# State products moved in a PE-bound scan and MLP kernel: ahead of the scans in the first group, into the y tile of the pair before in the later ones

## The chip, the cores and the metric

One core of one Trainium2 chip. The time is the device time of one execution in microseconds; the figure of a kernel is the median of its runs. A profile is one such execution, and its span is somewhat shorter than the execution's own time.

## The reference, cut to what matters

```python
# x (4, 8, 768, 32), a (4, 8, 768), B and C (4, 8, 768, 16); chunks of 32 steps
for c in range(nc):
    cum = np.cumsum(log(a) of the chunk)
    L = exp(cum_i - cum_j), causal
    y_intra = ((Cc @ Bc.T) * L) @ xc
    y_inter = (Cc @ state) * exp(cum)
    y[chunk] = y_intra + y_inter
    state = decay_full * state + sum_j(Bc_j xc_j * decay_from_j)
h = y_as_tokens(3072, 256) @ w_in          # (256, 2048)
g = maximum(h, 0) + alpha * minimum(h, 0)
out = g @ w_out                            # (2048, 256)
```

The result doesn't depend on the length of a chunk; the kernel takes 128 steps to a chunk. The weights arrive as 64-bit floats.

## The kernel before, in words

**Units of work.** There are 24 chunks of 128 steps (4 sequences of 6), taken two at a time: 12 pairs, `gp` 0 to 11. Two pairs make a group of 512 tokens, so there are six groups, and three pairs make a sequence. A pair first gives y for its 256 tokens; the MLP then runs on whole groups. In the third pair of each sequence (2, 5, 8, 11) only the first chunk's state is needed, since the sequence ends there.

**A pair** is a Python generator, `pair(gp)` (line 416). Each `yield` ends a step, and `ssm(gp, stages)` takes so many steps. In the order of the kernel before, for pairs 4 to 11 (`fine` is true there):

- transposes of B and C (L469), ACT's copy of them to `bc` (L472), and `bn`, B scaled by decays, by POOL (`pair_loads`, L385)
- four steps of decay scans on DVE (`half_decays`, L438), two scans each, with ACT's `spread_c` (L484: C spread to `cz`) in the fourth
- the state products (`added`, L519) on PE into a PSUM tile of their own, the state on DVE (`states`, L547), its masked copy `sm` on POOL (L550), and POOL's `c_decayed` (L487)
- Gram products of B and C (L564) and their multiplication with the decays on DVE (L600), in two steps
- y (L616 with the states, L623 with the decayed Gram), two PSUM tiles, each copied to `xts` by ACT (L630)

Pairs 0 and 1 start the kernel and have an order of their own. Pairs 2 and 3 run in the loop of the first group, with all scans of a chunk in one step; before, they have seven steps: transposes with `spread_c` and `bn`; scans of the first chunk; scans of the second; state products; Gram, first half; Gram, second half; y.

**The first group's MLP** is direct: `hidden` (L642, with ACT's multiply L645 and DVE's L646 as the PReLU) for each of 16 blocks of 128 columns, and `output` (L680). The first four blocks are taken in halves by `hidden_two` (L657, L663, L669). The loop over `f` from 4 to 15 runs, at each `f`, the steps of pairs 2 and 3, `hidden(0, f)`, one weight conversion, and `output(f - 4)`.

**The weights** come as 16 pieces of 512 KB, alternating `w_in` and `w_out` (piece 3 is the first of `w_out`, piece 4 serves blocks 6 and 7, piece 5 is the second of `w_out`). Of each, `convert_a` issues ACT's two reads of the raw piece (L218, L225 or L228) and POOL's clip (L220); `convert_b` two DVE operations (L238, L239); `convert` the add that finishes it (L261, mostly POOL). `convert_next` converts the next piece, issues `convert_a` for the piece after the next unless `first=False`, and issues the load of the piece six later on SP.

**The later groups** multiply by a seven-product scheme with sums: `quad(g, z, after)` takes four blocks at a time (z 0 to 3) in PSUM tiles A and Y (L766), PReLUs (L749, L751), POOL's differences (L800, L809), and `product` (L741) multiplies the quad before by `w_out`. It needs sums of weights (`weight_sums`, L709) and of tokens (`token_sums`, four operations on POOL, L721). `after(j)` is called at 14 places in a quad; a table, `steps`, says at which (z, j) a pair takes a step, and `ahead` at which `pair_loads` is called for a later pair. With `nxt = 2 * g + 2`, pairs `nxt` and `nxt + 1` are worked in group g's quads, for the group after.

**Order.** Every engine runs its instructions in the order in which the program issues them, so a place in the program is a place in each engine's queue. PSUM has eight banks: two for `ps_s` (tag `ss`), two for `ps_h` (tag `hp`: hidden tiles, A, Y, and spare ones), four `bank(i)` for outputs. In the first group `ss_tile` takes turns between the two of `ps_s` and `bank(2)`, once `bank(3)` holds an identity for the scans (`identity_bank`). The fourth Gram block of a pair takes an `hp` tile (`spare`).

Of the kernel before, what the change touches and what calls it, by code (L numbers as in the profile page):

```python
# [9 lines left out]
F32 = mybir.dt.float32  # L10
U32 = mybir.dt.uint32
U16 = mybir.dt.uint16
ALU = mybir.AluOpType
# [9 lines left out]
def kernel(  # L23
# [25 lines left out]
    nc = tc.nc  # L49
# [6 lines left out]
    P = 128  # L56
# [52 lines left out]
    def ss_tile():  # L109
        if early[0] is None:  # L110
            return ps_s.tile([P, 512], F32, name="ss")
        early[0] += 1
        i = early[0] % (3 if ident_p else 4)
        return ps_s.tile([P, 512], F32, name="ss") if i < 2 else bank(i)
# [211 lines left out]
    held = {}  # L326
    bns = {}

    def identity_bank():


        m5_bank.append(bank(3))
        nc.scalar.copy(out=m5_bank[0][:, HT:], in_=ident_h[:, :HT])
        ident_p.append(m5_bank[0][:, HT:])
# [42 lines left out]
    def pair_loads(gp):  # L377

        b, c = divmod(2 * gp, CPB)
        nat, abc, xt, ap = loads["p", gp]  # L380

        bn = work.tile([P, 2, H * N], F32, name="bn")
        i, bi = divmod(b, 2)
        pj = prt[i].rearrange("p (b h c) -> p b c h", b=2, h=H)[:, bi, c : c + 2]
        nc.gpsimd.tensor_tensor(  # L385
            out=bn.rearrange("p k (h n) -> p k h n", h=H),
            in0=nat[:, 0].rearrange("p k (h n) -> p k h n", h=H),
            in1=pj.unsqueeze(3).to_broadcast([P, 2, H, N]), op=ALU.mult)
        return bn
# [22 lines left out]
    def spare():  # L412

        return ps_h.tile([P, GT], F32, name="hp", tag="hp")

    def pair(gp):

        b, c = divmod(2 * gp, CPB)
        nat, abc, xt, ap = loads["p", gp]
        last = c + 2 == CPB  # L420
        dec = work.tile([P, 2, H, Q], F32, name="dec")
        dv = dec.rearrange("p k h t -> p k (h t)")

# [37 lines left out]
            yield  # L461


        tp = spare() if gp == 1 else ss_tile()
        if gp == 0:
            keep_warm(tp, 3, Q)
# [10 lines left out]
        def spread_c():  # L477
            for e in range(2):
                o = cz[:, e].rearrange("p k t -> p (k t)")
                if gp == 0 and e == 1:  # L480
                    nc.gpsimd.tensor_scalar(out=o, in0=ct, scalar1=par[:, e : e + 1],
                                            scalar2=None, op0=ALU.mult)
                else:
                    nc.scalar.mul(o, ct, par[:, e : e + 1])  # L484

        def c_decayed():
            nc.gpsimd.tensor_tensor(out=cd.rearrange("p k t -> p (k t)"), in0=ct, in1=pf,  # L487
                                    op=ALU.mult)

        fine = gp >= 2 * GC // 2  # L490
        if not fine:
            spread_c()
        if gp == 0:
            rows_turn(0, held.pop("pr"))
            dps = spare()
            keep_warm(dps, 6, Q)
            yield
        bn = bns.pop(gp) if gp in bns else pair_loads(gp)
        if gp == 1:
            c_decayed()  # L500
            dps = spare()
# [1 line left out]
        elif gp:  # L503
            yield

        nk = 1 if last else 2
        st = [masked.get(b)]  # L510
        new = work.tile([P, 2, P], F32, name="state")
        sm = work.tile([P, 2, P], F32, name="sm")

        def added(dps):
            dps = dps.rearrange("p (k m) -> p k m", m=P)
            for k in range(nk):
                for w in range(KC):
                    ws = slice(64 * w, 64 * w + 64)
                    nc.tensor.matmul(dps[ws, k], bn[:, k, ws], xt[:, k, w * P : (w + 1) * P],  # L519
                                     start=True, stop=True, tile_position=(0, 64 * w),  # L520
                                     skip_group_check=True)
            return dps

        if fine:
            for k in range(2):
                for w in range(2):
                    half_decays(k, w)
                    if k == 1 and w == 1:
                        spread_c()
                    yield  # L530
        else:
            decays(0)
            if gp == 1:
                dps = added(dps)
            if gp:
                yield
            if gp != 1:
                decays(1)

        def states(dps):  # L540
            for k in range(nk):
                old = state.get(b)
                if old is None:
                    nc.scalar.copy(out=new[:, k], in_=dps[:, k])
                else:
                    e = (k + 1) * Q - 1
                    nc.vector.scalar_tensor_tensor(out=new[:, k], in0=old, scalar=pf[:, e : e + 1],  # L547
                                                   in1=dps[:, k], op0=ALU.mult, op1=ALU.add)
                state[b] = new[:, k]
            nc.gpsimd.tensor_tensor(out=sm[:, :nk], in0=new[:, :nk],  # L550
                                    in1=hmask.unsqueeze(1).to_broadcast([P, nk, P]), op=ALU.mult)
            st.extend(sm[:, k] for k in range(nk))
            masked[b] = st[-1]

# [21 lines left out]
        if gp == 0:  # L578
            gram = products_bc()
            dps = added(dps)  # L580
            yield
            c_decayed()
            times(dec[:, :, :2], one_less(gram))
        elif gp == 1:
            decays(1)
            gram = products_bc()
            g0 = one_less(gram)
            states(dps)
            times(dec[:, :, :2], g0)
        else:  # L590
            if not fine:
                yield
            states(added(ss_tile()))
            c_decayed()
            yield
            gram = products_bc()
        for i, r in enumerate(r for r in ((2, 3, 0, 1) if fine else (3, 2, 1, 0) if gp > 1 else range(4))
                              if r in gram):
# [6 lines left out]
        yield  # L605


        y = [ss_tile()[:, : 2 * Q].rearrange("p (k t) -> p k t", k=2) for w in range(KC)]
        if gp < 2:
            keep_warm(y[0].rearrange("p k t -> p (k t)"), 2 - gp)  # L610
        begun = False
# [347 lines left out]
    prelus[1]()  # L959
    ssm(1)  # L960
    convert_a(*pieces[3])
    prelus = [hidden_two(0, 0, 2 * Q, spare())]
    prelus[0]()
    prelus = [hidden_two(0, 2, 2 * Q, spare())]
    convert_a(*pieces[4])
    convert_next(first=False)
    prelus[0]()
    identity_bank()
    convert_a(*pieces[5])
    convert_next()  # L970
    in_steps = {8: 0, 10: 1, 12: 2, 14: 3}
    for f in range(FIRST, NF):
        if f in (5, 10):
            load_pair(3 + f // 10)
        if f == 5:
            load_rows(1)
        if f == 9:
            rows_clamp(1)
            held["pr"] = rows_scan(1)
            rows_out(1)  # L980
        if f <= 10:
            ssm(2)
        if f >= 9:
            ssm(3)
        hidden(0, f)
        convert_next()
        output(f - FIRST)
        if f in in_steps:
            weight_sums(wi, in_sums, 0, in_steps[f])
    early[0] = None  # L990
    token_sums(1)
    ssm(2 * GC // 2, 2)


    steps = {(0, 1): 0, (0, 2): 0, (0, 5): 0, (0, 9): 0, (0, 13): 0, (1, 1): 0, (1, 5): 0,
             (1, 12): 1, (1, 14): 1, (2, 1): 1, (2, 2): 1, (2, 5): 1, (2, 9): 1, (2, 13): 1,
             (3, 1): 1, (3, 5): 1, (3, 12): 2, (3, 14): 2}

    late_sums = {(0, 2): ((wqt, out_sums, 0, 0),), (0, 4): ((wqt, out_sums, 0, 1),),
# [11 lines left out]
    for i in range(NZ * (NG - 1)):  # L1011
        g, z = divmod(NZ + i, NZ)
        nxt = 2 * g + 2

        def after(j, g=g, z=z, i=i, nxt=nxt):
            places = with_gram if nxt < NP and z % 2 == 0 else without
            if i and j in places:
                product(*divmod(NZ + i - 1, NZ), places[j])
            if i == 0:
                for f, half in last_out.get(j, ()):  # L1020
                    output(NF - LATE + f, half)
            if (i, j) in ((0, 13), (1, 8)):
                store_first(i)
            for w, sums, q0, part in late_sums.get((i, j), ()):
                weight_sums(w, sums, q0, part)
            if g > 1 and z == 0 and j in (5, 9, 13, 14):
                if j == 5:
                    comb[0] = combine(g - 1)
                next(comb[0], None)
            if g > 1 and z in (1, 3) and j == 11:  # L1030
                finish(g - 1, z // 2)
            if nxt + steps.get((z, j), NP) < NP:
                ssm(nxt + steps[z, j])
            if nxt < NP and (z, j) == (3, 7):
                token_sums(g + 1)
            ahead = nxt + {(1, 3): 1, (3, 8): 2}.get((z, j), NP)
            if ahead < NP:
                if ahead == 6:
                    rows_turn(1, held["pr"])
                bns[ahead] = pair_loads(ahead)  # L1040

        comb = [None] if i == 0 else comb
        if z == 0 and nxt < NP:
            load_pair(nxt + 1)
        if z == 2 and nxt + 2 < NP:
            load_pair(nxt + 2)
        quad(g, z, after)
# [31 lines left out]
```

## Time and profile before

| what | value |
|---|---|
| median of 10 runs | 378.34 us (377.33 to 379.7) |
| the profiled execution | 378.65 us |
| its span | 376.9 us |
| start of the loop over `f` on PE (hidden of block 4) | 31.21 us |
| first quad of the second group on PE | 86.24 us |

Each row of a group or of the timeline gives the engine, the source line, the operation, what is written and read, and the count. In the timeline the first two columns are start and duration in us, and the bracket at the end says how long the engine idled ahead of the row and on what. A row of waits gives the waiting engine and line, the releaser, the total in us, how often, and the longest.

### The profile page before, as it was taken

Reading aid. Unit: us, or ns where it says so; the run is one execution under the profiler, and the core shown is the slowest. Engines: PE = TensorE matmul, PEld = TensorE weight load, DVE = VectorE, ACT = ScalarE, POOL = GpSimd, SP = SyncE. Lnnn points to the kernel's source line nnn. Section 1 sums busy time; section 2 is a strip of 40 time slices with the busy share of each in tenths; the row PEclk is TensorE's granted clock in tenths of the full one; section 3 lists DMA queues with packets and bytes.
Section 4 is the critical chain, followed back from the end, with each engine's and each line's share of the span. In section 5 each row is a group of like instructions: output and inputs, shape, how many; then the busy total and the mean of one; then the engine's idle time right before and its main releaser. Section 6 shows DMA issues by size and latency. Waiting matters only on the chain.

```text
span 376.9 us, 6178 instructions
## 1 busy us (share of the span) xinstructions
PE 365.8 (97%) x2223; PEld 294.5 (78%) x2223; DVE 242.4 (64%) x461; ACT 179.7 (48%) x384; POOL 203.4 (54%) x212
## 2 busy tenths in 40 slices
PE   8898899999999999999999999999999999999996
PEld 7675466668778788788788788788788788888884
DVE  7884799967637737747737847647856734543364
ACT  1557766525354445545435535525625525543541
POOL 4875366779766846445456345356364355264512
PEclk9999999999999999999999999999999999999999
DMA  7989698831008801001801801801811000001003
GB/s 144 222 163 343 181 242 211 170 77 56 30 0 162 174 2 54 4 0 28 168 17 31 178 2 29 181 1 28 152 33 22 9 0 15 16 0 30 1 0 84
DMA packets 121879, 30.71 MB, mean 81 GB/s; under 512 B 93737, under 2 KB 117753, under 8 KB 121849
## 3 DMA queue, kind: packets, MB, share of 16 engines
q1 hardware_dynamic: 116736, 29.74, 35.7%
q10 hardware_dynamic: 5112, 0.59, 1.1%
q8 instruction: 17, 0.28, 0.3%
q14 instruction: 14, 0.11, 0.1%
HBM read 26.98 MB, written 3.34 MB: 80 GB/s over the span
## 4 chain that ended last, share of the span: by engine, by line
PE 87%; DVE 5%; DMA 2%; POOL 2%; ACT 2%; issue 1%; POOLq 0%; DVEq 0%; ACTq 0%
PE hp L766 33%; PE bank L741 32%; PE bank L680 5%; PE hp L642 3%; DMA raw<-in_moe_w_in_dram 2%; PE ss L623 2%; PE ss L564 2%; PE ss L616 1%; DVE dec L438 1%; PE ss L519 1%; PE hp L564 1%; PE hp L657 1%; PE ss L469 1%; PE hp L270 1%; DVE wr L239 1%
## 5 line engine op out<-in xcount | busy, mean ns | idle before, releaser
L809 POOL TENSOR_TENSOR gt<-gt 128x512 f32<-128x512 f32 x58 | 73.6, 1269 | 31.7 <-DVE gt L751 24.8
L751 DVE SCALAR_TENSOR_TENSOR gt<-hp,s_mul,gt 128x256 f32<-128x256 f32 x120 | 52.6, 480 | 47.7 <-ACT gt L749 46.7
L741 PE MATMUL bank<-gt,w_out 128*128 128x256 f32 x320 | 82.5, 382 | 0.4 <-ACT o_sb L687 0.4
L749 ACT ACTIVATE gt<-hp,s_alpha 128x256 f32<-128x256 f32 x120 | 50.3, 470 | 47.2 <-PE hp L766 32.9
L741 PEld LDWEIGHTS bank<-gt,w_out 128*128 128x128 f32 x320 | 60.0, 190 | 11.2 <-issue 2.3
L800 POOL TENSOR_TENSOR gt<-gt 128x512 f32<-128x512 f32 x20 | 25.4, 1270 | 78.3 <-DVE gt L751 78.3
L741 PE MATMUL bank<-gt,ws 128*128 128x256 f32 x240 | 58.3, 379 | 0.0
L741 PEld LDWEIGHTS bank<-gt,ws 128*128 128x128 f32 x240 | 45.1, 190 | 5.8
L438 DVE TENSOR_TENSOR_SCAN dec<-abc,bank 128x256 f32<-128x256 f32 x80 | 48.1, 661 | 0.0
L766 PE MATMUL hp<-xs,w_in 128*128 128x256 f32 x160 | 42.8, 390 | 0.0
L766 PE MATMUL hp<-xT,w_in 128*128 128x256 f32 x160 | 41.9, 384 | 0.0
L766 PE MATMUL hp<-xs,ws 128*128 128x256 f32 x160 | 41.1, 379 | 0.0
L785 DVE TENSOR_TENSOR hp<-hp,u 128x512 f32<-128x512 f32 x20 | 14.0, 700 | 39.6 <-ACT u L783 39.6
L774 ACT COPY m<-hp 128x512 f32<-128x512 f32 x20 | 11.7, 586 | 51.5 <-PE hp L766 51.5
L766 PEld LDWEIGHTS hp<-xs,w_in 128*128 128x128 f32 x160 | 28.7, 189 | 7.7 <-issue 3.3
L766 PEld LDWEIGHTS hp<-xs,ws 128*128 128x128 f32 x160 | 30.4, 190 | 4.1
L766 PEld LDWEIGHTS hp<-xT,w_in 128*128 128x128 f32 x160 | 29.7, 190 | 5.0 <-issue 1.4
L680 PEld LDWEIGHTS bank<-w_out,gt 128*128 128x128 f32 x128 | 24.1, 190 | 11.7 <-issue 4.9
L680 PE MATMUL bank<-w_out,gt 128*128 128x256 f32 x128 | 30.7, 381 | 2.3 <-POOL w_out L261 2.3
L789 DVE TENSOR_TENSOR c<-hp,m 128x512 f32<-128x512 f32 x20 | 13.6, 682 | 19.3 <-PE hp L766 19.3
L642 PE MATMUL hp<-xT,w_in 128*128 128x512 f32 x48 | 23.3, 607 | 0.7 <-DVE gt L646 0.7
L783 ACT COPY u<-hp 128x512 f32<-128x512 f32 x20 | 11.7, 585 | 23.0 <-PE hp L766 23.0
(155 smaller groups left out, 555.4 us busy)
## 6 DMA issues: line engine op xcount, KB each, us to landing
abc<-z SPq DMA_DIRECT2D x20, 512.0 KB, 5.0
raw<-in_moe_w_in_dram SPq DMA_DIRECT2D x8, 512.0 KB, 5.2
raw<-in_moe_w_out_dram SPq DMA_DIRECT2D x8, 512.0 KB, 6.9
xt<-in_x_dram SPq DMA_DIRECT2D x24, 128.0 KB, 3.2
out_dram<-o_sb SPq DMA_DIRECT2D x32, 64.0 KB, 1.9
nat<-in_B_dram SPq DMA_DIRECT2D x22, 64.0 KB, 2.8
nat<-in_C_dram SPq DMA_DIRECT2D x22, 64.0 KB, 3.6
ap<-pf SPq DMA_DIRECT2D x11, 128.0 KB
```

Of the source, the lines that this page charges most:

```text
L438: nc.vector.tensor_tensor_scan(out=dv[:, k, hs], data0=abc[k][:, hs], data1=ident_p[0], initial=0.0, op0=ALU.mult, op1=ALU.add)
L642: nc.tensor.matmul(hp, w_in[:, k, f * P : (f + 1) * P], xts[g][:, k], start=(k == 0), stop=(k == KC - 1))
L680: nc.tensor.matmul(pos[0][t // 2][:, t % 2], gt[:, t * Q : (t + 1) * Q], w_out[:, f], start=(f == 0 and t % 2 == 0), stop=(f == NF - 1), s ...
L741: nc.tensor.matmul(ms[g][i][:, h], w, blocks[g, z][n][:, p], start=(q == 0 and h == 0), stop=(q == NQ - 1), skip_group_check=True)
L749: nc.scalar.mul(o[:, p], h[:, p], s_alpha[:, fs[p]])
L751: nc.vector.scalar_tensor_tensor(out=o[:, p], in0=h[:, p], scalar=s_mul[:, fs[p]], in1=o[:, p], op0=ALU.mult, op1=ALU.max)
L766: nc.tensor.matmul(to[:, p], w(2 * z + p), b, start=start and p == 0, stop=True, skip_group_check=True)
L774: nc.scalar.copy(out=m1, in_=A)
L785: nc.vector.tensor_tensor(out=Y, in0=Y, in1=u2, op=ALU.add)
L789: nc.vector.tensor_tensor(out=c22, in0=A, in1=m5, op=ALU.add)
L800: nc.gpsimd.tensor_tensor(out=tc_, in0=g22, in1=g12, op=ALU.subtract)
L809: eng.tensor_tensor(out=o, in0=x0, in1=x1, op=ALU.subtract)
```

## The change

- Ahead of the loop, piece 3 is converted before the PReLUs of the first blocks' second halves are finished; the first part of piece 5 moves behind the multiply of hidden block 4 and that of piece 6 behind the conversion of piece 5; piece 7's comes at f = 5.
- `bn` of pairs 2 and 3 is made ahead, by calls of `pair_loads` before the loop and at f = 8.
- In pairs 2 and 3 the state products, the state and `c_decayed` come ahead of the scans of the first chunk, in the same step; `spread_c` comes behind the scans of the second. They have six steps in place of seven, and the calls of `ssm` stay as they are, so y comes one block earlier.
- The clamp, scans and writes of the rows of the second half of the sequences move from the head of f = 9 to behind the conversion at f = 11.
- In pairs 4 to 11 the state products, with state and mask, become the first step. Pairs 5 to 11 write them to the free half of the second y tile of the pair before (`beside`), and the step is taken directly behind that y. Pair 4 takes it at the end of the first group's loop, where now three steps are taken in place of two. `c_decayed` comes with the last scans, and the steps at j = 9 of the even quads go. `bn` is made at (0, 9) and (2, 9) in place of (1, 3) and (3, 8).

```diff
+    beside = {}
...
+        fine = gp >= 2 * GC // 2
...
+        if fine:
+            bn = bns.pop(gp) if gp in bns else pair_loads(gp)
+            states(added(beside.pop(gp) if gp in beside else ss_tile()[:, : 2 * Q]))
+            yield
...
         tp = spare() if gp == 1 else ss_tile()
...
-        if not fine:
+        if gp < 2:
             spread_c()
...
-        bn = bns.pop(gp) if gp in bns else pair_loads(gp)
+        if not fine:
+            bn = bns.pop(gp) if gp in bns else pair_loads(gp)
...
                     half_decays(k, w)
                     if k == 1 and w == 1:
                         spread_c()
+                        c_decayed()
                     yield
         else:
+            if gp > 1:
+                states(added(ss_tile()))
+                c_decayed()
             decays(0)
...
             if gp != 1:
                 decays(1)
+            if gp > 1:
+                spread_c()
...
             if not fine:
                 yield
-            states(added(ss_tile()))
-            c_decayed()
-            yield
             gram = products_bc()
...
-        y = [ss_tile()[:, : 2 * Q].rearrange("p (k t) -> p k t", k=2) for w in range(KC)]
+        ys = [ss_tile() for w in range(KC)]
+        y = [t[:, : 2 * Q].rearrange("p (k t) -> p k t", k=2) for t in ys]
+        if fine:
+            beside[gp + 1] = ys[1][:, 2 * Q :]
...
     convert_a(*pieces[3])
-    prelus = [hidden_two(0, 0, 2 * Q, spare())]
-    prelus[0]()
-    prelus = [hidden_two(0, 2, 2 * Q, spare())]
+    convert_next(first=False)
+    hidden_two(0, 0, 2 * Q, spare())()
+    rest = hidden_two(0, 2, 2 * Q, spare())
     convert_a(*pieces[4])
+    rest()
+    identity_bank()
+    bns[2] = pair_loads(2)
     convert_next(first=False)
-    prelus[0]()
-    identity_bank()
-    convert_a(*pieces[5])
-    convert_next()
...
-        if f == 9:
-            rows_clamp(1)
-            held["pr"] = rows_scan(1)
-            rows_out(1)
...
         hidden(0, f)
-        convert_next()
+        if f < FIRST + 2:
+            convert_a(*pieces[f + 1 + (f > FIRST)])
+        convert_next(first=f > FIRST)
+        if f == FIRST:
+            convert_a(*pieces[6])
+        if f == 8:
+            bns[3] = pair_loads(3)
+        if f == 11:
+            rows_clamp(1)
+            held["pr"] = rows_scan(1)
+            rows_out(1)
         output(f - FIRST)
...
     token_sums(1)
-    ssm(2 * GC // 2, 2)
+    ssm(2 * GC // 2, 3)
-    steps = {(0, 1): 0, (0, 2): 0, (0, 5): 0, (0, 9): 0, (0, 13): 0, (1, 1): 0, (1, 5): 0,
-             (1, 12): 1, (1, 14): 1, (2, 1): 1, (2, 2): 1, (2, 5): 1, (2, 9): 1, (2, 13): 1,
+    steps = {(0, 1): 0, (0, 2): 0, (0, 5): 0, (0, 13): 0, (1, 1): 0, (1, 5): 0,
+             (1, 12): 1, (1, 14): 1, (2, 1): 1, (2, 2): 1, (2, 5): 1, (2, 13): 1,
              (3, 1): 1, (3, 5): 1, (3, 12): 2, (3, 14): 2}
...
                 ssm(nxt + steps[z, j])
+
+            if j == 5 and z % 2 and nxt + z // 2 + 1 < NP:
+                ssm(nxt + z // 2 + 1)
...
-            ahead = nxt + {(1, 3): 1, (3, 8): 2}.get((z, j), NP)
+            ahead = nxt + {(0, 9): 1, (2, 9): 2}.get((z, j), NP)
```

## Prediction before the result

> **What bounds the kernel now.** I read the busy shares first, then the waits of TensorE (PE), then PE's and the other engines' order of time from 20 to 110 us.
>
> ```profile
> PE 365.8 (97%) x2223; PEld 294.5 (78%) x2223; DVE 242.4 (64%) x461; ACT 179.7 (48%) x384; POOL 203.4 (54%) x212
> ...
> PE 87%; DVE 5%; DMA 2%; POOL 2%; ACT 2%; issue 1%; POOLq 0%; DVEq 0%; ACTq 0%
> ```
>
> PE has no slack anywhere: 97% of the span, 87% of the chain that ended last. So an edit is worth the PE time that it adds or removes, and nothing else. PE's list of waits:
>
> ```profile
> PE bank L680 <- POOL w_out L261: 2.3, 2, 1.4
> PE hp L519 <- POOL bn L385: 1.7, 2, 1.4
> ...
> PE hp L642 <- DVE gt L646: 0.7, 1, 0.7
> PE ss L564 <- DVE state L547: 0.5, 1, 0.5
> PE bank L616 <- DVE dec L600: 0.4, 1, 0.4
> PE bank L741 <- ACT o_sb L687: 0.4, 1, 0.4
> ```
>
> In the order of time five of these lie in the loop of the first group: 1.45 us at 34.5, 0.69 at 40.7, 0.85 at 43.5, 0.48 at 50.6, 0.45 at 59.7; together 3.92. Pair 2's Gram products also stretch from 49.41 to 51.65, 2.24 us with the 0.48, where pair 3's take 1.08: 0.68 more. So 4.6 us can be won there. From 60 us on PE waits 0.44 us at 112.8 and hardly elsewhere.
>
> Three places decide the new waits. First POOL ahead of the second group (which starts on PE at 86.24):
>
> ```profile
> 82.55 1.26 POOL L261 TENSOR_TENSOR w_out<-wr,wg 128x512 uint32<-128x512 uint32 x1 [1.78 <-ACT xT L630]
> 83.77 1.27 POOL L709 TENSOR_TENSOR w_in<-w_in 128x512 f32<-128x512 f32 x1
> 85.00 0.73 POOL L721 TENSOR_TENSOR xs<-xT 128x256 f32<-128x256 f32 x1
> ...
> 87.86 0.64 POOL L385 TENSOR_TENSOR bn<-nat,prt 128x256 f32<-128x256 f32 x1
> ```
>
> Pair 4's scaled B (L385) comes behind the last conversion, a weight sum and four token sums, and ends at 88.50. Now it is read at 95.19. Second, the end of a pair, on PE and on ACT:
>
> ```profile
> 95.19 0.66 PE L519 MATMUL ss<-xt,bn 128*64 128x128 f32 x8
> 95.78 1.13 PE L766 MATMUL hp<-xT,w_in 128*128 128x256 f32 x4
> ...
> 106.75 1.08 PE L623 MATMUL ss<-dec,xt 128*32 128x128 f32 x32
> 107.76 1.13 PE L766 MATMUL hp<-xs,w_in 128*128 128x256 f32 x4
> ```
>
> ```profile
> 107.68 0.65 ACT L630 COPY xT<-ss 128x256 f32<-128x256 f32 x2 [1.69 <-PE ss L623]
> ```
>
> ACT reads the two y tiles until 108.33; PE has gone on at 107.76. Third, two halves of one PSUM bank, written by PE and read by ACT:
>
> ```profile
> 27.21 3.72 PE L657 MATMUL hp<-xT,w_in 128*128 128x256 f32 x16 [0.27 <-ACT xT L630]
> 30.77 0.60 PE L469 MATMUL bank<-ident,nat 128*128 128x128 f32 x4
> ```
>
> ```profile
> 30.97 0.84 ACT L663 ACTIVATE gt<-hp,s_alpha 128x256 f32<-128x256 f32 x2 [0.89 <-PE hp L657]
> ```
>
> The first half read here was finished about 0.9 us before 30.77, and ACT stood idle for 0.89; it started 0.20 us after the last matmul of the other half. So the program guards by bank and not by columns.
>
> **What the Trainium skill says.** "PSUM — Partial Sum Buffer", section "PSUM bank collisions raise a hardware error": two engines must not touch one bank in the same 32 partitions at the same time, disjoint columns included, so semaphores have to guard by bank. The wait at 30.97 agrees. "TensorEngine Tiling (Array Packing)", "Key Properties": changing the tiling mode drains TensorE. The trace agrees: L519 starts 0.10 late (95.09 would be on time), and the row behind it takes 0.97 to the next instead of 0.86. "TensorE: Matmul & The Clock Gate", Part 1: after an idle window of about 3.4 us the clock halves; no wait here is that long (longest 1.45), so the trace doesn't show it. "SBUF — State Buffer", "Who interferes with whom": DVE and GpSimd share a port pair that one holds for a whole instruction; L239 takes 0.69 us alone and 1.58 beside a POOL add at 33.5.
>
> **The change, part by part.**
>
> *Fourth piece (out columns 0) ahead of the PReLUs.* Its DVE half can run at 27.5 to 29.7, where DVE idles 2.54 us, and its POOL add ends at about 31.0 instead of 34.48. Output 0 can start at 33.10: minus 1.45.
>
> *First parts of pieces 5 to 7 behind hidden 4's PReLU.* ACT sits 1.69 us on piece 6's DMA (36.51) ahead of hidden 4's multiply at 39.07. Now the multiply comes at 33.7 (behind the copies of piece 4, the identity and bc), DVE's half at 34.4. The 0.69 and, since piece 5 is ready by 38.4 instead of 43.4, the 0.85 go. On SP, the load of piece 11 (40.92, held by piece 5's slot) and pair 3's loads behind it issue up to 5 us earlier; no PE wait hangs on them: zero.
>
> *B's products, state products ahead of scans, one step less.* POOL makes bn of pairs 2 and 3 (0.64 to 1.1 us each) before they are asked for. The products move from f=7 and 12 to f=5 and 10, the y's from f=10 and 15 to 9 and 14. The 0.48, the 0.68 and the 0.45 go. PE's work is the same.
>
> *What is late next.* Take T, when PE leaves hidden 14, with y of pair 3 ahead of it. PE passed from 33.10 (end of hidden 4) to 82.25 (start of hidden 15) in 49.15; less 3.92, 0.68 and output 10 (1.73, now behind T) that is 42.82, so T = 75.92 plus new waits. DVE has no slack there. (a) Pair 2's Gram takes an hp buffer at f=7, so hidden 7 needs hidden 6's buffer. DVE from 34.4: PReLU 0.65, second half of a conversion 1.35 (1.13 to 2.24 in the trace), state 0.35, four scans 2.4, PReLU 0.65, conversion 1.35, scans 2.4, PReLU 0.65: 44.2. PE without it: 33.1 and five halves of a step at 1.73, products 0.47, Gram 1.17: 43.4. Wait 0.8 (0.4 to 1.7). (b) The row scans (2.6 us on DVE, from 56.41 to 59) now stand at f=11, ahead of pair 3's Gram; hidden 13 needs that Gram's buffer. From the start of pair 3's state products, DVE: 1.5 to the state, 2.4, 0.65, 1.35, 2.4, 0.65, 1.35, 2.6, 0.6 = 13.5; PE: 0.79, three steps of 3.46, Gram 1.17 = 12.3. Wait 1.2 (0.5 to 1.7). (c) Behind it DVE needs 3.8 to the last Gram block, PE 3.55: 0.25 at y. Sum 2.3 (1.0 to 3.5): T = 78.2 (76.9 to 79.4). The rows' DMAs now queue on SP behind pair 4's loads; pair 6 reads them a group later: zero.
>
> *Pair 4's state products at the group's start.* The three steps taken at the end of the loop now begin with them. PE waits for bn, and transposes and the first quad are queued behind. POOL's row: PReLU of hidden 14 ends T+1.58 (84.08 to 85.66 for hidden 15), 1.35 to the add (81.20 to 82.55), add 1.22, sum 1.23, token sums 2.86, bn 0.64, signal 0.05: T+8.93 = 87.1. PE is there after outputs 10 and 11 and hidden 15, T+5.3 = 83.5. **Wait 3.6 us.** Then products 0.7 and transposes 0.44: the quad starts at 88.25 against 86.24, 2.0 later; the products at 95.19 (0.69 and 0.10 behind) are gone, minus 0.8. The first group therefore ends **1.2 later** (0 to 2.5), not earlier.
>
> *State products of pairs 5 to 11 behind y, in y's second tile.* Same bank, other columns. ACT copies y from that bank until 108.33, so by the guard above PE may write at 108.38, with the products, the rest of the quad and all outputs queued behind. Before, y and products took until 107.76+0.10 and 0.79: 108.65. Now 108.38+0.59+0.10 = 109.07. **0.42 a pair.** The other six y's repeat this (copy starting 0.08 before PE's next row, 0.65 long). For one-state pairs both sums are shorter by the same 0.22. Bounds: without the wait one drain less, worth about 0.18 (0.36 over ideal for the products' two switches), so -0.18; with ACT late, 0.6. Seven pairs: **+2.9** (-1.3 to 4.2).
>
> *The rest.* The state's DVE op (0.35 or 0.7) goes to where DVE idles 2.2 us for PE (108.93). bn at (0,9) and (2,9) costs POOL 0.64; pair 6's B is issued by 117.3 and (2,9) comes near 125.8, so it has landed; if not, some 7 us remain until its use. Scaled C waits beside scans. Zero.
>
> **Sum.** 1.2 + 2.9 = 4.1. The profiled execution (span 376.9, 378.65 with what lies around it) becomes 382.75; the median of the runs is 0.3 below that execution, 378.34, so 382.5.
>
> **Rivals.** (1) *No wait behind y*: the products run beside ACT's copies and seven drains are saved, -1.3. For it: columns are disjoint and the order is built to join them; against it: 30.97. Then 378.34+1.2-1.3 = 378.3, not slower; it decides at whether L519 starts before the copy ends. (2) *Clock*: the 3.6 us wait spans an idle window and PE runs at half speed for up to one window, 1.7 us more or twice that: 385. For it: the length; against it: the window must fall just so. (3) *bn is there sooner*: DVE's conversions run at 1.13, T near 77 and the bank wait at 0.3: the first group costs nothing and the rest 2.1, 380.4.
>
> **How the numbers follow.** The forecast, 70%: 382.5. Rival 1, 16%: faster 7, the same 7, slower 2. Rival 2, 6%; rival 3, 8%, both slower. A measurement tells 0.2% (0.76 us) from no change. Faster 7%, same 7%, slower 86%. The forecast's bounds are 380.4 to 385; two in ten left out, with part of rival 1 taken in, gives 379.2 to 385.0.
>
> **What would show it.** Right: PE waits of L519 on bn near 3.6 us before the first quad, and seven waits of L519 on ACT L630, about 0.5 each; the waits of L680 on w_out gone. Wrong: L519 starting less than 0.2 us behind L623, or bn ahead of the token sums; T far from 78.

## The result and the profile after

The changed kernel takes **387.78 us** (median of 9 runs, 387.53 to 388.94), the kernel before 378.29 (32 runs). The ratio is 1.0256, 95% interval 1.0240 to 1.0272: slower by 9.5 us. The forecast was 382.5, at most 385.0. The direction was right, the size less than half of it.

The profiled executions took 387.37 us (span 385.2) and 378.65 (span 376.9). Between their spans lie 8.3 us, and these are what the traces can explain. The other 1.2 us is how these two executions stand to the medians: before's was 0.4 above its median, after's 0.4 below, and 0.4 more lies around after's span.

The changed kernel's page, with busy shares, the chain's shares and the granted clock (the share of TensorE's full clock that it was given, here in tenths for 40 slices of the span):

```profile
PE 366.8 (95%) x2223; PEld 295.4 (77%) x2223; DVE 244.2 (63%) x461; ACT 179.4 (47%) x384; POOL 202.0 (52%) x212
...
PE 83%; DVE 7%; POOL 3%; issue 3%; ACT 2%; POOLq 0%; DVEq 0%; ACTq 0%
...
PEclk9999999998999999999999999999999999999999
```

PE is busy 1.0 us longer with the same 2223 instructions, and the clock has one slice of 8, at 87 to 96 us. The rest of the 8.3 us is idle time. PE's list of waits says where (lines have moved: L519 is now L478, L616 L629, L623 L636, L642 L655, L680 L693, L741 L754, L766 L779, ACT's L630 L643):

```profile
PE ss L478 <- issue: 4.2, 7, 0.6
PE ss L478 <- POOL bn L387: 3.6, 1, 3.6
PE hp L655 <- DVE gt L659: 2.7, 2, 1.7
...
PE hp L655 <- DVE dec L610: 0.8, 1, 0.8
```

The waits on `w_out` are gone. In their place stand three of hidden blocks, one of 3.6 us on `bn`, and seven of 0.6 in state products, which the profile puts to no engine ("issue"). In the order of time on PE, around the end of the first group and at the end of pair 4:

```profile
44.76 1.98 PE L655 MATMUL hp<-xT,w_in 128*128 128x512 f32 x4 [1.68 <-DVE gt L659]
67.36 1.95 PE L655 MATMUL hp<-xT,w_in 128*128 128x512 f32 x4 [1.01 <-DVE gt L659]
71.82 1.98 PE L655 MATMUL hp<-xT,w_in 128*128 128x512 f32 x4 [0.78 <-DVE dec L610]
78.71 1.89 PE L693 MATMUL bank<-w_out,gt 128*128 128x256 f32 x8
...
87.64 1.12 PE L478 MATMUL ss<-xt,bn 128*64 128x128 f32 x8 [3.60 <-POOL bn L387]
88.69 1.12 PE L509 MATMUL ss<-ident,nat 128*128 128x128 f32 x4
89.60 1.66 PE L779 MATMUL hp<-xT,w_in 128*128 128x256 f32 x4
91.10 1.03 PE L779 MATMUL hp<-xs,ws 128*128 128x256 f32 x4
...
110.09 1.08 PE L636 MATMUL ss<-dec,xt 128*32 128x128 f32 x32
111.77 0.44 PE L478 MATMUL ss<-xt,bn 128*64 128x128 f32 x4 [0.60 <-issue]
112.14 1.13 PE L779 MATMUL hp<-xs,w_in 128*128 128x256 f32 x4
```

T, the row at 78.71, was forecast at 78.2. The three rows above it with a wait are hidden blocks 7, 12 and 13. The wait on `bn` is the 3.6 us of the forecast to the tenth. What was not in the sum: behind it the products take 1.05 to the next row, the transposes 0.91, the quad's first row 1.50, where full speed gives 0.59, 0.44 and 0.86. That is 1.57 us. The clock in these stretches (columns: stretch, its length, busy time of PE, PEld, DVE, ACT, POOL, granted clock, DMA share, GB/s):

```profile
86.00:88.00 2.00, 0.36 (x4) 0.36 (x6) 0.00 (x0) 0.00 (x0) 1.59 (x3) 0.86 0.00 0
88.00:90.00 2.00, 2.00 (x13) 1.61 (x10) 1.15 (x3) 0.15 (x1) 0.31 (x1) 0.50 0.00 0
90.00:92.00 2.00, 2.00 (x9) 1.66 (x8) 2.00 (x5) 1.02 (x2) 1.92 (x3) 0.78 0.00 0
```

So the rival "clock", given 6%, came true on top of the forecast. At the pair's end y's last matmul would have been done near 111.17; the products start at 111.77, behind ACT's copy of the two y tiles:

```profile
111.02 0.65 ACT L643 COPY xT<-ss 128x256 f32<-128x256 f32 x2 [1.69 <-PE ss L636]
```

From the start of L636 of pair 4 (110.09 after, 106.75 before) to that of pair 8 (228.54 and 222.41), after needs 118.45 us and before 115.66: **0.70 a pair**, where the forecast had 0.42. By y itself, all seven pairs add 5.0 us (each 0.65 to 0.77), and pair 4's y starts 3.34 later. 3.34 and 5.0 are the 8.3 us.

### The profile page after: what moved, and what is told of

Read it like the earlier page. It is cut to its first block, busy times and chain, and to the rows that moved or that the text cites. A ratio compares the mean times of both kernels' runs of the same rounds, so it can differ in the third digit from the quotient of the medians.

```text
span 385.2 us, 6165 instructions
## 1 busy us (share of the span) xinstructions
PE 366.8 (95%) x2223; PEld 295.4 (77%) x2223; DVE 244.2 (63%) x461; ACT 179.4 (47%) x384; POOL 202.0 (52%) x212
## 3 DMA queue, kind: packets, MB, share of 16 engines
HBM read 26.98 MB, written 3.34 MB: 79 GB/s over the span
## 4 chain that ended last, share of the span: by engine, by line
PE 83%; DVE 7%; POOL 3%; issue 3%; ACT 2%; POOLq 0%; DVEq 0%; ACTq 0%
PE hp L779 33%; PE bank L754 31%; PE bank L693 3%; PE hp L655 2%; DVE dec L441 2%; PE ss L636 2%; PE hp L670 2%; PE ss L577 2%; PE ss L629 1%; PE ss L478 1%; PE ss L509 1%; DVE gt L659 1%; PE hp L577 1%; DVE wr L239 1%; PE hp L270 1%
## 5 line engine op out<-in xcount | busy, mean ns | idle before, releaser
L754 PE MATMUL bank<-gt,w_out 128*128 128x256 f32 x320 | 82.5, 382 | 0.4 <-ACT o_sb L700 0.4
L754 PEld LDWEIGHTS bank<-gt,w_out 128*128 128x128 f32 x320 | 60.0, 190 | 11.2 <-issue 2.3
L754 PE MATMUL bank<-gt,ws 128*128 128x256 f32 x240 | 58.3, 379 | 0.0
L754 PEld LDWEIGHTS bank<-gt,ws 128*128 128x128 f32 x240 | 45.1, 190 | 5.8
L779 PE MATMUL hp<-xs,w_in 128*128 128x256 f32 x160 | 42.8, 390 | 0.0
L779 PE MATMUL hp<-xT,w_in 128*128 128x256 f32 x160 | 42.5, 389 | 0.1
L779 PE MATMUL hp<-xs,ws 128*128 128x256 f32 x160 | 41.1, 379 | 0.0
L779 PEld LDWEIGHTS hp<-xT,w_in 128*128 128x128 f32 x160 | 30.2, 193 | 6.7 <-ACT hp L808 2.9
L779 PEld LDWEIGHTS hp<-xs,w_in 128*128 128x128 f32 x160 | 28.7, 189 | 7.5 <-issue 2.8
L779 PEld LDWEIGHTS hp<-xs,ws 128*128 128x128 f32 x160 | 30.4, 190 | 4.2
L693 PEld LDWEIGHTS bank<-w_out,gt 128*128 128x128 f32 x128 | 24.2, 190 | 8.7 <-issue 6.1
L693 PE MATMUL bank<-w_out,gt 128*128 128x256 f32 x128 | 30.5, 380 | 0.0
L493 POOL TENSOR_TENSOR sm<-state,bmask 128x256 f32<-128x256 f32 (+1 forms) x12 | 7.6, 636 | 38.8 <-DVE state L490 36.6
L655 PE MATMUL hp<-xT,w_in 128*128 128x512 f32 x48 | 23.2, 605 | 3.5 <-DVE gt L659 2.7
```

Of the source, the lines that this page charges most:

```text
L655: nc.tensor.matmul(hp, w_in[:, k, f * P : (f + 1) * P], xts[g][:, k], start=(k == 0), stop=(k == KC - 1))
L693: nc.tensor.matmul(pos[0][t // 2][:, t % 2], gt[:, t * Q : (t + 1) * Q], w_out[:, f], start=(f == 0 and t % 2 == 0), stop=(f == NF - 1), s ...
L754: nc.tensor.matmul(ms[g][i][:, h], w, blocks[g, z][n][:, p], start=(q == 0 and h == 0), stop=(q == NQ - 1), skip_group_check=True)
L779: nc.tensor.matmul(to[:, p], w(2 * z + p), b, start=start and p == 0, stop=True, skip_group_check=True)
```

## The experiments

The theory: three causes add up. The wait on `bn` costs 3.6 us and another 1.5 by the clock; the guard by bank costs 0.6 at each of seven pair ends; and the products taken away inside the quads give back less than they took, since they had covered a hole, a short stretch in which PE would otherwise have waited. Rivals: the clock is harmless or no part of it; the 0.6 is the switch of the tiling and no guard; the loss per pair lies in the table of steps; the first group's part is itself a loss. The fall of the clock lies ahead of pair 4's y, so a pair's cost is read below from the first L636 rows of pairs 4 and 8, behind it:

| kernel | L636 of pair 4, us | from pair 4 to 8, us | a pair against before, us |
|---|---|---|---|
| before | 106.75 | 115.66 | 0 |
| after | 110.09 | 118.45 | +0.70 |
| pair 4's `bn` sooner | 105.28 | 118.45 | +0.70 |
| y's first tile | 111.91 | 117.36 | +0.43 |
| two places later | 111.54 | 116.02 | +0.09 |
| product moved into the hole | 110.36 | 120.98 | +1.33 |
| hole filled | 110.40 | 118.59 | +0.73 |
| first group's part alone | 105.29 | 115.74 | +0.02 |
| later part alone | 107.93 | 118.47 | +0.70 |

**Pair 4's `bn` sooner.** Changed kernel, with one call more in the loop:

```diff
+        if f == 13:
+            bns[4] = pair_loads(4)
```

> The changed kernel, with pair 4's bn made by POOL at f = 13, ahead of the last conversion and the token sums. My theory (the first quad waits 3.6 us for bn behind POOL's queue, and the clock halves in that wait, which costs about 1.5 more): both go, minus 5.1 us against the changed kernel, 382.7. Rival (bn is only the last of several things that POOL owes the quad): the wait moves on to the token sums' readers, L779, and less than 1.5 us comes back, 386.3 or more.

382.45 us, ratio to before 1.0122 (1.0102 to 1.0143). Its PE at the same place:

```profile
84.28 0.66 PE L478 MATMUL ss<-xt,bn 128*64 128x128 f32 x8
...
85.36 1.03 PE L779 MATMUL hp<-xT,w_in 128*128 128x256 f32 x4
```

No wait and full clock. The products start 3.36 us sooner than in the changed kernel, pair 4's L636 comes 4.81 sooner: the 1.45 between them is the clock. The four executions have mean clocks of 0.998 to 1.0, all those of the changed kernel 0.991 to 0.996. The place of one POOL instruction of 0.64 us, behind an add, a weight sum and four token sums, had cost 5.3 us of the median.

**The wait filled, twelve calls and six.** Multiplications of no use, into the tile that the products then write, added ahead of them for pair 4:

```diff
-            states(added(beside.pop(gp) if gp in beside else ss_tile()[:, : 2 * Q]))
+            to = beside.pop(gp) if gp in beside else ss_tile()[:, : 2 * Q]
+            if gp == 4:
+                keep_warm(to, 12)
+            states(added(to))
```

> The changed kernel, with 12 extra matmuls of 128x256 by ones (2.6 us) in the wait ahead of pair 4's state products; they write the tile that these products then overwrite. Clock theory: bn comes at the same time, about 87.6 us, but TensorE is not idle long enough to be slowed, and the products, the transposes and the first four matmuls of the quad take 0.6, 0.44 and 0.9 in place of 1.05, 0.9 and 1.5: minus 1.5 us, 386.3. Rival (a restart after a wait is slow whatever the clock): no change, 387.8.

387.99 us, ratio 1.0266 (1.0243 to 1.0289): no gain, where 386.3 was expected. The filler was too long:

```profile
83.50 5.34 PE L270 MATMUL ss<-warm 128*128 128x256 f32 x24
88.77 0.66 PE L478 MATMUL ss<-xt,bn 128*64 128x128 f32 x8
...
90.72 1.03 PE L782 MATMUL hp<-xs,ws 128*128 128x256 f32 x4
```

Twelve calls are 24 passes and 5.34 us, so the products start 1.1 us later than in the changed kernel; yet the quad's second row starts 0.4 earlier (90.72 to 91.10). The median alone says nothing of the clock, since the filler spent what the clock gave back. With 6 in place of 12:

> The changed kernel, with 6 extra matmuls of 128x256 by ones (12 passes of 0.22, 2.6 us) in the wait of 3.6 us ahead of pair 4's state products, half of what overfilled it. Clock theory: bn ends the wait as before, but at full clock: minus 1.4 us, 386.4. Rival: no change, 387.8.

386.23 us, ratio 1.0226 (1.0207 to 1.0244).

```profile
84.34 2.75 PE L270 MATMUL ss<-warm 128*128 128x256 f32 x12
...
88.13 0.66 PE L478 MATMUL ss<-xt,bn 128*64 128x128 f32 x8 [1.03 <-POOL bn L387]
...
89.21 1.03 PE L782 MATMUL hp<-xT,w_in 128*128 128x256 f32 x4
```

The products still wait for `bn`, and start 0.5 us later than in the changed kernel, as this whole execution is 0.5 later from pair 3's y on. But they and the two rows behind them take 1.95 to the quad's second row (90.08) instead of 3.46. The clock's part is 1.5 us, and it is the idle stretch that brings it on: behind a wait of 1.03 us the rows have full speed, so a restart alone isn't slow.

**y's first tile.** The products written beside the y tile that ACT copies first:

```diff
-            beside[gp + 1] = ys[1][:, 2 * Q :]
+            beside[gp + 1] = ys[0][:, 2 * Q :]
```

> The changed kernel, with the state products of pairs 5 to 11 in the free half of the first y tile, which ACT copies first, in place of the second. Bank theory (TensorE waits until ACT has read y out of that bank): the seven waits shorten by the distance of the two copies, 0.27 us, from 0.60 to about 0.33: minus 1.9 us, 385.9. Rival (the wait is the price of changing from y's matmuls to the products, as its row names no engine but issue): 0.60 stays, 387.8.

385.92 us, ratio 1.0220 (1.0196 to 1.0245). Its waits:

```profile
PE ss L478 <- issue: 2.2, 7, 0.3
```

Only the bank changed, and the wait fell from 0.60 to 0.32, 0.28 a pair as in the table (0.70 to 0.43). A switch of the tiling would have cost the same in either tile; it is the bank that ACT reads.

**Two places later.** The step behind y taken at j = 7 of the odd quads instead of j = 5:

```diff
-            if j == 5 and z % 2 and nxt + z // 2 + 1 < NP:
+            if j == 7 and z % 2 and nxt + z // 2 + 1 < NP:
```

> The changed kernel, with the step of the state products at j = 7 of the odd quads in place of directly behind y at j = 5; the tile is the same. Bank theory: ACT has long read y, so the seven waits of 0.60 go, and one change of tiling mode of 0.1 to 0.2 us comes back a pair: minus 3 us, 384.8. Rival (the products cost this wherever they stand): no change, 387.8.

384.08 us, ratio 1.0171 (1.0147 to 1.0195). PE never waits there:

```profile
144.35 0.66 PE L478 MATMUL ss<-xt,bn 128*64 128x128 f32 x8
```

The table's 0.09 flatters this version, though. Between the y's of pairs 4 and 5 the kernel before and the changed one each wait 0.44 us for ACT (the row at 117.16 in the changed kernel, `bank` L754 on `o_sb` L700); here the products run in that time, and this interval is 0.37 shorter than before. The six intervals behind it are each 0.18 to 0.30 longer than before, and all seven add 1.16 us in place of 5.0. So most of the later part's loss hangs on the place of one step: at j = 5 everything behind the products waits with them. The 0.2 to 0.3 that stays is about what the even quads don't give back (below).

Pair 4's L636 comes at 111.54, 1.45 later than in the changed kernel, since the clock of this execution stayed down longer:

```profile
88.00:90.00 2.00, 2.00 (x13) 1.67 (x12) 1.05 (x3) 0.05 (x1) 0.21 (x1) 0.50 0.00 0
90.00:92.00 2.00, 2.00 (x6) 1.55 (x6) 2.00 (x5) 0.88 (x2) 1.92 (x3) 0.50 0.00 0
92.00:94.00 2.00, 2.00 (x7) 1.61 (x6) 1.14 (x2) 0.83 (x2) 2.00 (x3) 0.58 0.44 134
```

**A product moved into the hole.** The Gram step's product 7, in the table of steps at j = 11, taken at j = 9, where the state products had been:

```diff
-    with_gram = {3: 1, 5: 2, 7: 3, 8: 5, 11: 7, 13: 6, 14: 4}
+    with_gram = {3: 1, 5: 2, 7: 3, 8: 5, 9: 7, 13: 6, 14: 4}
```

> The changed kernel, with the even quads' third matmul group of w_out (product 7) at j = 9, where the state products stood before, in place of j = 11, as the odd quads have it. Cover theory (before, part of the state products' time lay beside a wait of 0.2 to 0.3 us, in which the first matmuls of b21 wait until ACT has copied m1 back into Y; with the products gone that wait is bare): it is covered again in seven quads, minus 1.5 to 2 us, 386.0. Rival (the rest of the loss per pair lies elsewhere): no change, 387.8.

392.27 us, ratio 1.0368 (1.0343 to 1.0392): a miss, the wrong way. A new wait appears, not there in the changed kernel:

```profile
PE hp L577 <- DVE gt L764: 2.8, 7, 0.4
```

The last Gram block takes an `hp` buffer; with product 7 ahead, it comes while DVE's PReLU still holds that buffer. So the time says nothing for or against the hole, but the rows at the place do:

```profile
219.61 1.03 PE L779 MATMUL hp<-xs,w_in 128*128 128x256 f32 x4
220.47 1.03 PE L754 MATMUL bank<-gt,w_out 128*128 128x256 f32 x4
221.34 1.03 PE L779 MATMUL hp<-xT,w_in 128*128 128x256 f32 x4
222.20 1.03 PE L754 MATMUL bank<-gt,ws 128*128 128x256 f32 x4
```

The first three take 2.59 us, full speed; in the changed kernel, with product 7 last of the three, they take 2.88 (from 217.38, shown below, to 220.26). The hole was filled, for 0.29; the Gram behind it then lost 0.86, 0.40 of this in the new wait.

**The hole filled.** One small multiplication of no use at j = 9 of the even quads:

```diff
+            if j == 9 and z % 2 == 0 and nxt < NP:
+                keep_warm(ss_tile(), 1, Q)
```

> The changed kernel, with one extra matmul of 128x128 by ones (two passes, 0.22 us) at j = 9 of the eight even quads of groups 1 to 4, where the state products stood before; nobody reads its tile. Cover theory (the changed kernel leaves 0.25 to 0.3 us bare there, while ACT copies m1 back into Y): the extra work fits in and costs nothing, 387.7. Rival (TensorE has no such hole): plus 8 x 0.22 = 1.7 us, 389.5.

387.95 us, ratio 1.0272 (1.0251 to 1.0292), against 387.78 for the changed kernel; 0.73 a pair for 0.70 (0.14 more in the first pair, nothing in the six behind it). So two passes of 0.22 us on PE cost nothing there: PE had stood idle. The place in the kernel before, then in the changed kernel:

```profile
210.97 1.03 PE L766 MATMUL hp<-xs,w_in 128*128 128x256 f32 x4
211.93 0.44 PE L519 MATMUL ss<-xt,bn 128*64 128x128 f32 x4
212.30 1.13 PE L766 MATMUL hp<-xT,w_in 128*128 128x256 f32 x4
213.27 1.03 PE L741 MATMUL bank<-gt,w_out 128*128 128x256 f32 x4
```

```profile
217.38 1.03 PE L779 MATMUL hp<-xs,w_in 128*128 128x256 f32 x4
218.43 1.13 PE L779 MATMUL hp<-xT,w_in 128*128 128x256 f32 x4
219.40 0.81 PE L754 MATMUL bank<-gt,w_out 128*128 128x256 f32 x3
```

And ACT in the changed kernel:

```profile
217.79 0.59 ACT L808 COPY hp<-m 128x512 f32<-128x512 f32 x1 [0.23 <-DVE gt L764]
```

Before, from 210.97 to 213.27 are 2.30 us with the products in them. After, without them, the same stretch takes 2.02, where two rows at full speed need 1.72: the row at 218.43 adds to what ACT's copy writes (until 218.38) and waits for it. So products that stood at 0.58 on PE gave back 0.28. Before, they ran while PE would have waited for ACT. This holds in all eight even quads: in the changed kernel the row starts 0.05 us after ACT's copy ends and its releaser is ACT L808; before, the copy had ended 0.32 to 0.65 us ahead of it.

**The first group's part alone.** The kernel before with the changed loop of the first group and the changed order of pairs 2 and 3; pairs 4 to 11 as before (the state products in the quads, two steps at the loop's end):

```diff
-        if fine:
-            bn = bns.pop(gp) if gp in bns else pair_loads(gp)
-            states(added(beside.pop(gp) if gp in beside else ss_tile()[:, : 2 * Q]))
-            yield
...
+            if fine:
+                states(added(ss_tile()))
+                c_decayed()
+                yield
```

> The first group's part of the change alone: pieces, bn of pairs 2 and 3, state products ahead of scans, rows at f = 11; pairs 4 to 11, their tables and the end of the loop as in the kernel before. My ledger: hidden 14 ends at 78.7 as in the changed kernel, the first quad starts at 84.4 in place of 86.24 without waiting for bn: minus 1.5 to 1.8 us against before, 376.4. Rival (the first group's part is worth nothing, since its own new waits of 3.5 us eat what it saves): 378.0.

377.28 us (22 runs), ratio 0.9977 (0.9965 to 0.9989): faster by 0.9 us, where 1.5 to 1.8 was expected. In the profiled execution L636 of pair 4 is 1.46 us ahead of before's. So the first group's edits are a small gain. Pair 4's products at the loop's end turn it into a loss by their wait for `bn` and the clock behind it: with `bn` sooner, L636 of pair 4 comes at 105.28, as here.

**The later part alone.** The changed kernel with the loop of the first group and pairs 2 and 3 as before:

```diff
-    convert_next(first=False)
-    hidden_two(0, 0, 2 * Q, spare())()
-    rest = hidden_two(0, 2, 2 * Q, spare())
+    prelus = [hidden_two(0, 0, 2 * Q, spare())]
+    prelus[0]()
+    prelus = [hidden_two(0, 2, 2 * Q, spare())]
...
```

> The later part alone: pairs 4 to 11 as in the changed kernel, the first group's order as before. My ledger: TensorE comes to pair 4's products at 85.8, bn at about 88.5, a wait of 2.7 us that is too short for the clock; less 0.5 for the products that leave the quad, and 7 x 0.71 for the pairs behind: plus 7.5, 385.6. Rival (the two parts spoil each other, and each alone does little): less than 382.

387.01 us, ratio 1.0234 (1.0205 to 1.0263), 1.4 above the expectation. Its profiled execution took 385.03:

```profile
86.99 0.66 PE L478 MATMUL ss<-xt,bn 128*64 128x128 f32 x8 [2.60 <-POOL bn L387]
```

Here the wait is 2.6 us, the clock stays full behind it, and pair 4 is 1.18 late. The mean granted clock of this execution is 0.999; the other five have 0.991 to 0.995 and spans 1.0 to 3.5 us longer. So a wait of 2.6 us can go without a fall; whether it is this wait that brings it on in the other five, no trace shows. A fall needn't come from this wait: two other profiled executions (y's first tile, and the last run below) have one ahead of the loop, and 4 of the 22 executions of the first group's part alone, which has no such wait, have a mean clock of 0.995.

**Better orders of the first group.** First the part alone, with the second rows at f = 8 instead of f = 11:

```diff
-        if f == 11:
+        if f == 8:
             rows_clamp(1)
```

> The first group's part alone, with the rows' clamp and scans at f = 8 in place of f = 11. DVE idles 3.8 us there while TensorE works at y of pair 2, so the 2.6 us of scans cost nothing and leave the queue ahead of pair 3's Gram: the waits of hidden 12 (1.0) and hidden 13 (0.8) go. 1.5 us less than the first group's part alone, 374.9, below both kernels. Rival (the wait moves to DVE's next late step): the same as that part alone, 376.4.

376.17 us, ratio 0.9940 (0.9920 to 0.9960): 1.1 us less than that part alone, where 1.5 was expected. Then with this, one `yield` more in pairs 2 and 3, between scans and Gram, which sends the Gram and y one block later:

```diff
             if not fine:
                 yield
+                yield
```

> The first group's part alone with the rows at f = 8, and with one more step in pairs 2 and 3 between the scans and the Gram products, so that these and y come a block later, as in the kernel before. My reason (the Gram's spare hp tile makes hidden 7 and 12 wait 1.6 and 1.0 us for the PReLU just ahead): a block later that PReLU is done, the waits go, and 2.6 us less than with the rows alone, 373.6. Rival (DVE is as late a block later, at y or at another hidden block): 376.2.

375.25 us, ratio 0.9932 (0.9912 to 0.9953), where 373.6 was expected. PE's waits with the rows at f = 8, then with the Gram later too:

```profile
PE hp L651 <- DVE gt L655: 2.7, 2, 1.6
```

```profile
PE bank L626 <- DVE dec L609: 0.6, 1, 0.6
```

The move of the rows took the 0.8 of hidden 13 away, and only that: hidden 12's 1.0 was not theirs. The later Gram took both waits of hidden blocks and left 0.6 at a y; the loop fell from 51.86 to 49.71 us (its start to the transposes of pair 4). The median fell by 0.9 only, and the intervals of the two ratios overlap, so this last gain is not clear of noise. In the profiled execution the loop began 1.6 us later; its granted clock was 0.50 from 13.57 to 16.99 us, ahead of anything that was changed here. This is the lowest median, by its ratio 2.6 us below the kernel before. It leaves the whole later part of the change out.

## Why the prediction was right in direction and wrong in size

Two steps failed. The sum booked the full time of the products taken out of the even quads as won, and it left the clock behind the wait of 3.6 us out. By the prediction's own steps, from the spans (8.3 us where it had 4.1):

- *The stalls removed, and T.* Right in sum, in part by luck. T came at 78.71 for 78.2 forecast. The new waits were 1.68 at hidden 7 (0.8 in the text), 0.78 at hidden 13 (1.2) and 1.01 at hidden 12 (none); y of pair 3 waited for nothing, where it had 0.25. Together they are 3.47 for 2.3, at the end of the range; without them PE was 0.7 ahead of the 75.92 forecast, 0.26 of it since this execution's loop began sooner (30.95 for 31.21). The term is 0.5 too small.
- *Pair 4's wait on `bn`.* Right, 3.60 for 3.6, and with it POOL's queue as read there.
- *"T+8.93", then "the quad starts at 88.25 … 2.0 later".* The step failed where it took full speed behind the wait. The quad's second row came 3.99 us later than before: 2.0 forecast, 0.5 from T, 1.57 of clock, less 0.1 in the products' own time. "Clock" stood among the rivals, beside the forecast and not in it, at 6%, since "the window must fall just so". It fell so in each of the five profiled executions with a wait of 3.6 us (the changed kernel, and the runs with y's first tile, the step two places later, the moved product and the filled hole). Kept from idling, PE lost nothing (the run with six calls: 1.5 us back). Its size, "1.7 us more or twice that", was right: 1.5 to 1.7 in four of the five, and 2.9 in the run two places later. Its chance was not.
- *"The products at 95.19 are gone, minus 0.8".* Nearly right: 0.59 came back at the place itself, where PE then waits for ACT's copy, and 0.66 in all up to pair 4's y. "The first group therefore ends 1.2 later" became 3.3.
- *"0.42 a pair".* Here the step failed that took "y and products … 108.65", that is, the products' full time, as won. The guard cost nearly what was foreseen: for two states the row behind the products starts 1.25 us later than before, where the text's own figures give 1.21 (108.38 + 0.59 for 107.76), for one state 1.04 for 0.99. But of the 0.79 us (two states) or 0.58 (one state) taken out of the even quads only 0.49 to 0.54 or 0.27 to 0.38 came back there, since the products had covered a wait for ACT's copy. That is 0.71 a pair, 5.0 in all for 2.9; 0.3 of the 2.1 between them is the guard's, the rest the products'. The bounds −1.3 to 4.2 did not hold it, since both counted the products' full time as won.
- *The rest.* Zero, as it was.

The sum of the misses: 0.5 for T, 1.5 for the clock, 2.1 for the pairs and 0.1 at 95.19: 4.2 of the 4.2 that the spans differ by. What stays open is the 1.2 us between spans and medians, which these traces don't show, and how often the clock falls behind a wait of 2.6 us.

Rival 1 (no wait behind y) is refuted: the products start 0.10 us after ACT's copy ends, and the run with y's first tile moves the wait by its bank alone. Rival 3 (`bn` sooner) is refuted by the 3.60.

## What to carry to other kernels

An instruction taken out of a full engine is worth its time only if the next one is ready: look at what the row behind it reads and when that lands, before its time is booked as won. A step moved to directly behind the last write of a PSUM tile waits for that tile's reader, in other columns too; two places later the wait was gone, and the step cost its own time of 0.57 to 0.78 us. And where the reading finds one wait of several us on TensorE, its consequences for the clock belong in the forecast, while a small instruction asked for sooner in the queue that makes it late takes away both.

## What the runs showed of the hardware that was not expected

The clock fell after a single wait of 3.6 us, to 0.50 in a stretch of 2 us behind it, in all five profiled executions with that wait; in the changed kernel its price was 1.5 us. The half clock lasted 3.41 us there (87.46 to 90.87), 3.4 in three others, and twice that, 6.83 us (86.86 to 93.69), in the run two places later. It needn't begin within the wait: in the run with the hole filled it began at 88.80, 1.05 us after PE had gone on. The Trainium skill, "TensorE: Matmul & The Clock Gate", Part 1, gives an idle window of about 3.4 us, and the five falls behind a wait of 3.6 agree with it, as does the wait of 2.6 with which the profiled execution kept its clock. But two profiled executions (y's first tile, and the one with the later Gram) also have 3.4 us of half clock ahead of the loop, where PE's longest waits were 1.91 and 2.08 us. So in these runs the length of one wait doesn't settle whether the clock falls.

Keeping PE busy there won nothing when the filler was too long: twelve calls over 256 columns in f32 ran as 24 passes of 0.22 us.
